# Attention heads laid as 64 partitions by 7 rows, on four 64x64 tiles of TensorE

## The chip, the cores and the metric

One core of one Trainium2 chip. The metric is the device time of one execution in microseconds (us), as the median of several; smaller is better. All runs told of here can be compared with one another. Each is set against runs of the kernel before in the same rounds.

## The reference

A cosine-similarity attention over 8 batches, 12 heads, 448 positions and 64 dimensions, followed by a two-layer perceptron with GELU over 3584 rows:

```python
q_n = q / (norm(q) + 1e-6);  k_n = k / (norm(k) + 1e-6)        # over the 64 dimensions
scores = q_n @ k_n.T / tau                                     # 448 x 448 per head
attn = exp(scores - max) / (sum + 1e-9)
x = (attn @ v), heads side by side: 3584 rows x 768
out = gelu(x @ w_in) @ w_out                                   # 768 -> 2048 -> 768
```

## The kernel before

Every batch has two stages. In the **attention stage** the heads go in pairs, each head's 448 positions as 112 partitions by 4 rows. GpSimd squares q and k and multiplies them by reciprocal norms, DMA transposes the result (TensorE does so in batch 0), TensorE makes scores, ScalarE exponentials, TensorE row sums and values, VectorE the division. Between groups of scores TensorE works off pieces of the second layer of earlier batches, the filler. The **first-layer stage** multiplies by `w_in`, and ScalarE makes the GELU. The parts that matter here:

```python
def scores(g, c0, n=2):                       # two heads = two row tiles of 64, keys in chunks of 112
    for c in range(c0, c0 + n):
        for h in range(2):
            nc.tensor.matmul(st[:CS, h, :S], lhsT=qkT[rows(h), 1, c, :], rhs=qkT[rows(h), 0, :, :], ...)
        nc.scalar.activation(pt, st[:CS, :, :S], AF.Exp, scale=inv_tau)

def columns(g, n, ...):                       # n=0: row sums; n=1, 2: odd and even halves of v
    ...                                       # four column tiles of 32: (head pair j, head h)
    nc.tensor.matmul(bank_t[g, n][r:r + 32, :S], lhsT=w, rhs=pt_t[g + j, c][:, h, :], tile_position=(0, r))

def reciprocals(g):
    nc.vector.transpose(tr, sums)             # 32x32 blocks
    nc.vector.reciprocal(rc, tr[:, :, 0])
    nc.vector.transpose(rs, rc.to_broadcast(...))

def normalise(g):
    for n in (2, 1):                          # the bank borrowed from the filler is freed first
        nc.vector.tensor_tensor(x_t[b][:, p + n - 1, :], bank_t.pop((g, n))[:, :S], rs, ALU.mult)

# attention stage, cut: filler of 96 or 128 matmuls in pieces, 16 to a bank, two banks by turns
plan = {96: ((18, 8), (8, 8), (0, 10), (8, 8), (0, 10), (8, 10)), 128: ...}
...
if i in (2, 4): both(g - 2, ...)              # sums, reciprocals, values, normalise
upto(reduce, ...)                             # next batch's squares: behind the normalising
```

## Time and profile before

| | before |
|---|---|
| median | 438.94 us (438.43 to 439.7) |
| TensorE busy | 428.9 us, 98% of the span |
| ScalarE, GpSimd, VectorE busy | 264.4, 204.3, 164.6 us |
| first layer of batch 0 starts at | 38.9 us |
| from one first layer to the next | 48.8 us (odd batches), 53.6 to 54.1 (even) |

TensorE's busy share is the first thing to read, and then whether it waits: in the waits of the kernel before (total us, times, longest), its longest wait after 60 us is 0.2 us:

```profile
PE hp L433 <- DVE x L246: 0.2, 1, 0.2
```

The chain of work is therefore a price list of TensorE's pieces. Those lines are in the prediction.

### The profile page before, as it was taken

The page shows a single profiled execution, that of the slowest core. Times are in us where ns is not written, and L with a number is a line of the kernel's source. Part 1 is how long each engine was busy: PE and PEld are TensorE (multiplying, and loading weights), DVE is VectorE, ACT ScalarE, POOL GpSimd, SP SyncE. Part 2 cuts the span into 40 slices and gives each one's busy share as a digit, 9 for nine tenths or more (in the row PEclk, how much of TensorE's full clock was granted, in tenths as well). Part 3 has the DMA queues.
Part 4 walks back from the last instruction along what each step waited for, and adds up shares of the span by engine and source line. Part 5 has one row for each costly group of instructions (what it writes and reads, how often), then busy time and mean ns, then how long its engine had stood idle before and what let it go on. Part 6 is the DMA issues. An engine that isn't in the chain of part 4 may idle for free.

```text
span 438.5 us, 7921 instructions
## 1 busy us (share of the span) xinstructions
PE 428.9 (98%) x3291; PEld 216.1 (49%) x3291; DVE 164.6 (38%) x266; ACT 264.4 (60%) x380; POOL 204.3 (47%) x185
## 2 busy tenths in 40 slices
PE   8899999999999999999999999999999999999996
PEld 4344544445444554455544545445444554445563
DVE  5667313642255305542154501753055421341021
ACT  4696587646766467754767359655766457773300
POOL 3989934491834609291571906655190732300000
PEclk9699999999999999999999999999999999999999
DMA  8999999945683907756195743858077600711022
GB/s 204 250 247 206 196 137 208 264 100 147 99 168 86 212 23 115 170 106 162 24 158 139 154 113 48 173 125 207 1 130 152 134 2 1 132 43 31 1 72 72
DMA packets 83635, 54.97 MB, mean 125 GB/s; under 512 B 41872, under 2 KB 78608, under 8 KB 83600
## 3 DMA queue, kind: packets, MB, share of 16 engines
q1 hardware_dynamic: 66416, 42.35, 43.0%
q0 software_dynamic: 16784, 11.80, 18.5%
q8 instruction: 25, 0.41, 0.4%
q10 hardware_dynamic: 400, 0.33, 0.2%
q14 instruction: 10, 0.08, 0.1%
HBM read 45.61 MB, written 11.01 MB: 129 GB/s over the span
## 4 chain that ended last, share of the span: by engine, by line
PE 93%; DVE 2%; ACT 2%; POOL 1%; DMA 1%; issue 0%; DVEq 0%; POOLq 0%
PE op L268 35%; PE hp L433 33%; PE st L206 12%; PE o L228 8%; PE sm L228 4%; ACT pt L209 1%; POOL qkb L176 1%; DMA qk<-in_q_dram 1%; PE spin L323 1%; PE tp L192 1%; DVE x L246 0%; DVE nq L147 0%; DVE nq L149 0%; ACT lq L155 0%; POOL v L120 0%
## 5 line engine op out<-in xcount | busy, mean ns | idle before, releaser
L209 ACT ACTIVATE pt<-st 112x896 bf16<-112x896 f32 x192 | 165.2, 913 | 49.6 <-PE st L206 49.2
L268 PE MATMUL op<-wo,g 128*128 128x384 bf16 x896 | 158.0, 327 | 0.0
L433 PE MATMUL hp<-x,wi 128*128 128x448 bf16 x768 | 147.0, 353 | 0.2 <-DVE x L246 0.2
L455 ACT ACTIVATE g<-hp 128x448 bf16<-128x448 f32 x128 | 67.0, 545 | 89.9 <-PE hp L433 89.5
L268 PEld LDWEIGHTS <-g 128*128 128x128 bf16 x896 | 81.8, 98 | 70.1 <-issue 21.0
L433 PEld LDWEIGHTS <-wi 128*128 128x128 bf16 x768 | 74.3, 98 | 72.3 <-issue 3.6
L176 POOL TENSOR_TENSOR qkb<-qk,rn 112x512 bf16<-112x512 f32 x95 | 97.8, 1055 | 11.3 <-DVE rn L167 11.0
L137 POOL TENSOR_TENSOR sq<-qk 112x1024 f32<-112x1024 f32 x44 | 82.3, 1888 | 5.8 <-DMA qk<-in_k_dram 5.7
L165 POOL TENSOR_SCALAR se<-sr 112x48 f32<-112x48 f32 x14 | 4.6, 326 | 150.0 <-ACT sr L164 150.0
L149 DVE TENSOR_REDUCE nq<-sq 112x16 f32<-112x1024 f32 x47 | 56.9, 1213 | 37.3 <-POOL sq L137 37.3
L206 PE MATMUL st<-qkT 64*112 64x448 bf16 x384 | 60.9, 380 | 1.9 <-ACT pt L209 1.7
L279 DVE COPY ot<-op 128x384 f32<-128x384 f32 x55 | 29.8, 542 | 79.3 <-PE op L268 79.3
L167 DVE RECIPROCAL rn<-se 112x48 f32<-112x48 f32 (+1 forms) x20 | 7.8, 392 | 99.7 <-POOL se L165 99.4
L228 PE MATMUL o<-pt,v 112*32 112x448 bf16 x768 | 41.4, 353 | 0.2 <-DVE x L246 0.2
L206 PEld LDWEIGHTS <-qkT 64*112 64x112 bf16 x384 | 21.7, 126 | 38.4 <-issue 34.9
L246 DVE TENSOR_TENSOR x<-o,rs 128x448 bf16<-128x448 f32 x48 | 27.7, 619 | 4.3 <-PE o L228 2.0
L235 DVE STREAM_TRANSPOSE tr<-sm 128x448 f32<-128x448 f32 x24 | 15.5, 647 | 35.5 <-PE sm L228 35.5
L228 PEld LDWEIGHTS <-v 112*32 112x32 bf16 x768 | 20.3, 97 | 16.0 <-issue 1.1
L228 PE MATMUL sm<-pt,ones 112*32 112x448 bf16 x384 | 23.1, 355 | 0.0
L239 DVE STREAM_TRANSPOSE rs<-rc 128x448 f32<-128x448 f32 x24 | 15.5, 645 | 0.8
L323 PE MATMUL spin<-blank,ident 112*112 112x448 bf16 x43 | 14.1, 483 | 1.5 <-POOL ident masks.py:199 1.3
L120 POOL DMA_DIRECT2D v<-in_v_dram x17 | 14.0, 822 | 0.0
(37 smaller groups left out, 80.6 us busy)
## 6 DMA issues: line engine op xcount, KB each, us to landing
qk<-in_q_dram SPq DMA_DIRECT2D x48, 224.0 KB, 5.9
qk<-in_k_dram SPq DMA_DIRECT2D x47, 224.0 KB, 6.1
v<-in_v_dram POOLq DMA_DIRECT2D x15, 336.0 KB, 6.9
wi<-in_moe_w_in_dram POOLq DMA_DIRECT2D x4, 768.0 KB, 9.6
wo<-in_moe_w_out_dram POOLq DMA_DIRECT2D x4, 768.0 KB, 16.9
out_dram<-ot SPq DMA_DIRECT2D x7, 336.0 KB, 3.6
out_dram<-ot SPq DMA_DIRECT2D x8, 288.0 KB, 2.6
out_dram<-ot SPq DMA_DIRECT2D x8, 240.0 KB, 2.7
```

The source lines that it names most:

```text
L137: nc.gpsimd.tensor_tensor(sq, t, t, ALU.mult)
L149: nc.vector.tensor_reduce(nq, sq, mybir.AxisListType.X, ALU.add)
L176: eng.tensor_tensor(qkb[:, i].rearrange("p c h d -> p h c d"), t[:, i], rn[:, i].to_broadcast([CS, 2, NC, D]), ALU.mult)
L206: nc.tensor.matmul(st[:CS, h, :S], lhsT=qkT[rows, 1, c, :], rhs=qkT[rows, 0, :, :], start=True, stop=True)
L209: nc.scalar.activation(pt, st[:CS, :, :S], AF.Exp, scale=inv_tau)
L228: nc.tensor.matmul(bank_t[g, n][r:r + 32, :S], lhsT=w, rhs=pt_t[g + j, c][:, h, :], start=(c == 0), stop=(c == NC - 1), tile_position=(0, r))
L246: nc.vector.tensor_tensor(x_t[b][:, p + n - 1, :], bank_t.pop((g, n))[:, :S], rs, ALU.mult)
L268: nc.tensor.matmul(ps[:, :NH], lhsT=g_t[sb][:, kf, t * 128:(t + 1) * 128], rhs=wo[:, kf, ni * NH:(ni + 1) * NH], start=(kf == 0), stop=(kf ...
L279: nc.vector.tensor_copy(ot[:, lo:hi], ps[:, :NH])
L323: nc.tensor.matmul(ps[:CS, :S], lhsT=ident, rhs=blank, start=True, stop=True)
L433: nc.tensor.matmul(hps[m], lhsT=wi[:, kd, m * 128:(m + 1) * 128], rhs=x_t[b][:, kd, :], start=(kd == order[0]), stop=(kd == order[-1]))
L455: nc.scalar.activation(g_t[sb][:, m, hf * S:(hf + 1) * S], hps.pop(m), AF.Gelu)
```

## The change

Its intent: a head's positions become 64 partitions by 7 rows, so that two heads fill 128 partitions. Four heads (a quad) then fill the array as four 64x64 tiles, both in the scores and in the values, with all 128 lanes of ScalarE and no partition idle. A sum of a head lands in two 32-partition quadrants, one for even and one for odd key chunks, so VectorE must add the halves of neighbouring quadrants. The core of it, cut:

```diff
-    CS = S // 4                                   # 112 partitions x 4 rows, pairs of heads
+    C = S // D                                    # 64 partitions x 7 rows, quads of heads
 def scores(...):
+        for n, (s, c) in enumerate(banks):
+            for h in range(2):
+                nc.tensor.matmul(st[cols, n, :S], lhsT=qkT[rows, 1, c, cols], rhs=qkT[rows, 0, :, cols],
+                                 start=True, stop=True, tile_position=(64 * s, 64 * h))
+    def sums(g, chunks=range(C)):                 # ones: columns 0-15 for rows 0-63, 16-31 for rows 64-127
+                r = 32 * (2 * s + c % 2)
+                nc.tensor.matmul(bank_t[g, "sm"][r:r + 32, :S], lhsT=ones, rhs=pt_t[g, s, c], ...)
+    def values(g, chunks=range(C), aside=0):
+                    nc.tensor.matmul(bank_t[g, h][cols, :S], lhsT=v_t[g][rows, s, c, :],
+                                     rhs=pt_t[g, s, c][rows], tile_position=(64 * h, 64 * s), ...)
 def reciprocals(g):
     transpose -> tr
+        for j in range(4):
+            nc.vector.tensor_copy(sw[32 * j:32 * (j + 1)], sums2[32 * (j ^ 1):32 * ((j ^ 1) + 1)])
+        nc.vector.tensor_tensor(su, sums2, sw, ALU.add)
+        nc.vector.reciprocal(rc, su)
+        for h in range(2): transpose rc[:, h] -> rs       # two instead of one
 def normalise(g):
-        for n in (2, 1):
+        for h in range(2):                        # the filler's bank is freed last
 attention stage:
+        plan = {96: (0, 18, 8, 8, 8, 0, 8, 8, 0, 8, 8, 22), 128: (0, 22, 12, 12, 12, 0, 12, 12, 0, 12, 12, 22)}
+            if i in (5, 8): both(...)
+            group(b, i)
+            if i in (4, 9): upto(reduce, ...)     # at 4: ahead of the first sums
```

(Cut: loads, stores and `w_in` in the new order, quad-sized squares and scaling, and the schedule of batch 0.)

## The prediction

> **What bounds the kernel now.** I read the page's busy table first, then the chain of work that ended last, in order of time, then the timelines of single engines around one attention batch. The page:
>
> ```profile
> PE 428.9 (98%) x3291; PEld 216.1 (49%) x3291; DVE 164.6 (38%) x266; ACT 264.4 (60%) x380; POOL 204.3 (47%) x185
> ...
> PE 93%; DVE 2%; ACT 2%; POOL 1%; DMA 1%; issue 0%; DVEq 0%; POOLq 0%
> ```
>
> TensorE is the bound: busy 98% of the span and 93% of the chain. Only the first batch, up to 38.97 us, has other links in the chain. So a change pays by taking matmul time out, and costs by making TensorE wait. The chain inside one later batch (number 3 of 0 to 7) gives the prices:
>
> ```profile
> 160.06 0.52 PE st L206 x4
> 160.57 3.03 PE op L268 x18
> 163.61 0.52 PE st L206 x4
> 164.12 1.41 PE op L268 x8
> ...
> 170.24 0.87 PE sm L228 x16
> 171.10 1.51 PE o L228 x32
> 172.62 0.52 PE st L206 x4
> 173.13 1.73 PE op L268 x10
> ```
>
> The 32 value matmuls take 1.51 us: four column tiles at once make 8 rounds of 0.189 us, a 448-column matmul's time. The 16 row sums take 0.87, 4 rounds (0.76) and 0.11. A score group of 4 (two row tiles, 2 rounds, 0.38) takes 0.52, so 0.14 over; 8 output-projection matmuls (`op`) take 1.41, 1.30 and 0.11. Every change of tile shape thus costs 0.11 to 0.14 us. The `op` matmuls of the previous batches are the filler between score groups, and they accumulate 16 to a bank, in two banks by turns.
>
> VectorE and GpSimd are not the bound, but two of their chains run close behind TensorE. VectorE after the first row sums of batch 3:
>
> ```profile
> 171.16 0.65 DVE L235 STREAM_TRANSPOSE tr<-sm 128x448 f32<-128x448 f32 x1 [3.19 <-PE sm L228]
> 171.84 0.24 DVE L237 RECIPROCAL rc<-tr 128x14 f32<-128x14 f32 x1
> 172.12 0.65 DVE L239 STREAM_TRANSPOSE rs<-rc 128x448 f32<-128x448 f32 x1
> 172.87 1.16 DVE L246 TENSOR_TENSOR x<-o,rs 128x448 bf16<-128x448 f32 x2
> 173.94 1.21 DVE L149 TENSOR_REDUCE nq<-sq 112x16 f32<-112x1024 f32 x1
> ```
>
> The sums start at 170.16 in TensorE's timeline, so `tr` starts 1.00 us later and both normalising multiplies are over 3.87 us after the start. The first multiply frees the bank that the next filler chunk needs; the reduction of the next batch's squares is issued only after them. And GpSimd in the same stretch:
>
> ```profile
> 165.21 2.04 POOL L176 TENSOR_TENSOR qkb<-qk,rn 112x512 bf16<-112x512 f32 x2 [0.57 <-DVE rn L167]
> 167.20 0.83 POOL L120 DMA_DIRECT2D v<-in_v_dram  x1
> 168.04 2.05 POOL L176 TENSOR_TENSOR qkb<-qk,rn 112x512 bf16<-112x512 f32 x2
> 170.05 1.89 POOL L137 TENSOR_TENSOR sq<-qk 112x1024 f32<-112x1024 f32 x1
> ```
>
> Its scaling starts 5.15 us after the attention batch (160.06), released by the reciprocal norms; 512 elements take 1.0 us start to start and 1024 squares 1.85.
>
> **What the Trainium skill says.** "TensorEngine Tiling (Array Packing)", Key Properties: changing the tiling mode drains the engine. The trace agrees: 0.11 to 0.14 us at each change. "TensorE: Matmul & The Clock Gate", Part 3: row and column tiles compose and run at once. The trace shows either kind alone at full overlap (rows in the scores, columns in the values), not both together. The same page, Part 1: an idle time over a free-running window of about 3.4 us can halve the clock. The trace's granted clock did fall, to 0.70 between 15 and 25 us, after the sparse first scores. "VectorE: DVE Perf Modes", Two Vector instructions with no wait between them: an instruction whose input or output starts in another 32-partition quadrant than the last one's is held until earlier ones finish. The kernel before has no such copies, so it cannot show this; the change adds four in a row.
>
> **The change, part by part.**
>
> TensorE. Two heads by four 112-key chunks become four heads by seven 64-key chunks. Per batch, scores go from 24 rounds to 21 and values from 24 to 21, if four 64x64 tiles run at once. Score groups: before 12 of 0.52 = 6.24 us; after ten of 0.52 and one of one round, 0.33, = 5.53: −0.71. One filler piece fewer: −0.11. Sums: 14 matmuls on four column tiles still need 4 rounds: 0. Values: 7 rounds are 1.32, plus a new shape change after the sums (0.11) and some exposed weight loading (0.03, estimated): 1.46 against 1.51, −0.05, three times. Together about −1.0 us per batch, −7 us for batches 1 to 7.
>
> ScalarE: 168 exponentials of 128x896 for 192 of 112x896 at 913 ns, −22 us of busy time. It is hidden behind TensorE in batches 1 to 7 but counts in batch 0: three fewer at 0.82 us back to back is −2.4. Against it, GpSimd now works on whole quads there (scaling 896 elements: 1.75 us by 512 -> 1.0; squares of 1792: 3.25), and the second quad's scaling ends later. I take batch 0 as −1 ± 2.
>
> VectorE after the sums. The first transpose stays (0.65 + 0.03). New: four copies of 28 elements across quadrants, one addition, a reciprocal of 28 instead of 14, a second transpose. The trace has a reduction from 32 to 16 elements at 179 ns and a 16-element reciprocal at 253 ns; I estimate 0.22 start to start for each held copy and for the addition, and 0.36 for the reciprocal (253 ns for 16 and 452 ns for 48 give 6.2 ns per element). Then 0.60 and 0.72 for two transposes and 1.16 for two multiplies. From the sums' start: 1.00 + 0.68 + 0.88 + 0.22 + 0.36 + 0.60 + 0.72 + 1.16 = 5.62 us, against 3.87.
>
> **Where that meets TensorE.** Values of the second head in each pair go to the idle filler bank, which is the one the next chunk of `op` needs, and it is now freed by the last multiply, not the first. In odd batches the filler has used 18+8+8+8 = 42 matmuls when the first sums come and 58 at the second: each time 6 are left to a multiple of 16. In even batches it is 22+36 = 58 (6 left) and 82 (14 left). From the sums' start TensorE needs 0.87 + 1.46 + 0.52 and 6 x 0.163 = 0.98, so at 3.83 us it wants the bank, which comes at 5.67 with the semaphore. **A wait of 1.84 us**, twice in odd batches and once in even ones (with 14 left TensorE wants it after 5.7 us or later). The kernel before escaped it: its first multiply ended at 3.3 against about 3.9.
>
> Worse, the reduction of the next batch's first squares now stands ahead of the first `tr` in VectorE's order. On batch 3's clock: scaling 165.1 to 168.6 (2 x 1.75), squares to 171.9, reduction (1792 elements, 2.02 us by 1213 ns for 1024) to 174.0. `tr` wanted to start at 171.1, so it is 2.9 us late and **the first wait of an odd batch is 4.8 us**. In an even batch the longer filler starts the sums about 2.3 us later (16 more matmuls by 0.163, less 0.3 for the groups' waits), `tr` is some 0.6 late, and the wait is 2.4. At the batch's end, 16 first-layer matmuls (3.03 us) stand between values and the last operands: 0.87 + 1.46 + 0.11 + 3.03 = 5.47 against 5.67, perhaps 0.1 to 0.2 lost.
>
> Sum: four odd batches x (4.8 + 1.84 + 0.15) = 27.2; three even x (2.4 + 0.15) = 7.7. Minus 7, minus 1: +27. 438.9 + 27 = **466 us**. A wait of 4.8 us may also halve the clock for some microseconds, four times; I put that into the range, not into the number.
>
> **Rivals.** (1) The matmul saving alone decides: about 431 us, −1.9%, if VectorE's chain kept ahead. For it: TensorE's 93% of the chain. Against it: 3.83 against 5.67 us, a margin that no plausible copy cost closes; copies at half the price still leave 1.4. (2) Only the bank waits occur, without the late reduction, because squares finish earlier than I think: 11 x 1.84 + 1 − 8 gives about 453. Against it: GpSimd's start is set by the roots, whose place in the order does not change. (3) Four tiles do not overlap fully, since two column tiles with different moving data share 64 rows: rounds up to doubled would add 42 x 0.19 = 8 us per batch, so 500 or more. Against it: four column tiles with four moving operands already overlap. I give it 5%.
>
> **Range and chances.** 466 with 8 in 10 between 448 and 480: the low end is rival 2 with cheaper copies, the high end colder clocks and dearer copies. Faster by over 2% needs both waits absent and a good batch 0: 0.06. Within 2%: 0.10. Slower: 0.84.
>
> **What will show it.** Right: `op` waiting for `x` about eleven times, four of them near 5 us; `tr` released by the reduction rather than the sums in odd batches; VectorE 5 us from `tr` to the last multiply's end where nothing is in the way; seven score rounds of 0.19 per quad; ScalarE near 242 us. Wrong: `op` never waiting for `x`, squares done before the first sums, or a score group over 0.6 us, which would mean tiles one after another.

## The result

The outputs are correct. **The changed kernel takes 536.02 us (median of 4, 534.5 to 537.71) against 439.27 us for the kernel before in the same rounds: ratio 1.220, 95% interval 1.217 to 1.223.** A ratio here is the mean time of one kernel's runs over that of the other's in the same rounds, so it is not quite the ratio of the medians. The direction was forecast, the size was not: 536 lies far outside 448 to 480.

The changed kernel's page (busy time, granted clock in 40 slices, then groups with busy us, mean ns and the idle time ahead of them):

```profile
PE 439.4 (82%) x3428; PEld 211.9 (40%) x3428; DVE 243.7 (46%) x387; ACT 242.9 (46%) x351; POOL 171.5 (32%) x113
PEclk9568999888999899797999989979799998999999
L451 PE MATMUL hp<-x,wi 128*128 128x448 bf16 x768 | 161.6, 373 | 34.1 <-DVE x L266 34.1
L287 PE MATMUL op<-wo,g 128*128 128x384 bf16 x896 | 162.8, 333 | 31.1 <-DVE x L266 31.1
L253 DVE COPY sw<-tr 32x28 f32<-32x28 f32 x96 | 72.3, 753 | 1.8
```

TensorE has fallen from 98% to 82%, and two groups of matmuls now wait 34 and 31 us for the normalised values `x`. VectorE has 79 us more work, and 72 of them are the four small copies: 753 ns for 28 elements. The clock granted to TensorE (`PEclk`, in tenths of full speed), full in the kernel before from the third slice on, dips all along. The waits (total us, times, longest):

```profile
PE hp L451 <- DVE x L266: 34.1, 6, 5.7
PE op L287 <- DVE x L266: 31.1, 11, 5.1
```

Eleven filler waits were forecast, the longest of about 5 us. The six of 5.7 us before the first layer were not. One of them, first in TensorE's timeline (start, length, times, idle time ahead), then in VectorE's, then in GpSimd's:

```profile
171.65 0.93 PE L230 MATMUL sm<-pt,ones 128*32 128x448 bf16 x14
172.52 1.52 PE L241 MATMUL o<-pt,v 64*64 64x448 bf16 x28
173.97 3.20 PE L451 MATMUL hp<-x,wi 128*128 128x448 bf16 x16
182.86 3.68 PE L451 MATMUL hp<-x,wi 128*128 128x448 bf16 x9 [5.69 <-DVE x L266]
```

```profile
172.63 0.65 DVE L249 STREAM_TRANSPOSE tr<-sm 128x448 f32<-128x448 f32 x1 [0.31 <-PE sm L230]
173.31 7.18 DVE L253 COPY sw<-tr 32x28 f32<-32x28 f32 x4
180.53 0.20 DVE L255 TENSOR_TENSOR su<-tr,sw 128x28 f32<-128x28 f32 x1
```

```profile
170.69 6.63 POOL L187 TENSOR_TENSOR qkb<-qk,rn 128x896 bf16<-128x896 f32 x4 [0.62 <-DVE rn L176]
177.28 3.17 POOL L147 TENSOR_TENSOR sq<-qk 128x1792 f32<-128x1792 f32 x1
```

Four copies of 28 elements take 7.18 us while GpSimd works through its scalings and a set of squares. The single copies take 0.75, 1.63, 1.64 and 3.11 us: each but the first is about one GpSimd instruction long, and each ends 0.03 to 0.05 us after a GpSimd instruction does. In the last batch GpSimd has nothing to do, and the same four take:

```profile
476.09 0.65 DVE L249 STREAM_TRANSPOSE tr<-sm 128x448 f32<-128x448 f32 x1 [3.50 <-PE sm L230]
476.78 0.75 DVE L253 COPY sw<-tr 32x28 f32<-32x28 f32 x4
```

The account of the profiled runs, 532.7 against 438.5 us: batch 0 takes 16.8 us more (its first layer starts at 55.7), the filler waits are 31.1, the first-layer waits 34.1, and 90 first-layer and filler matmuls after 35 us started at about half the usual rate, 15.2 us in all. Seven batches of saved matmuls are −7 (the forecast; run 9 below bears it out). That makes 90 of 94.

### The profile page after: what moved, and what is told of

It reads as the page before. It is cut to its first block, busy times and chain, and to the rows that moved or that the text cites. A ratio compares the mean times of both kernels' runs of the same rounds, so it can differ in the third digit from the quotient of the medians.

```text
span 532.7 us, 8122 instructions
## 1 busy us (share of the span) xinstructions
PE 439.4 (82%) x3428; PEld 211.9 (40%) x3428; DVE 243.7 (46%) x387; ACT 242.9 (46%) x351; POOL 171.5 (32%) x113
## 4 chain that ended last, share of the span: by engine, by line
issue 44%; PE 23%; POOL 21%; DVE 8%; DMA 2%; ACT 1%; SPq 0%; POOLq 0%; DVEq 0%
PE hp L451 10%; POOL sq L147 10%; POOL qkb L187 9%; PE op L287 8%; DVE sw L253 4%; PE st L216 2%; PE o L241 1%; PE sm L230 1%; DMA qk<-in_k_dram 1%; ACT pt L220 1%; DVE rs L260 1%; POOL v L127 1%; DVE nq L157 1%; DVE x L266 1%; DVE tr L249 1%
## 5 line engine op out<-in xcount | busy, mean ns | idle before, releaser
L220 ACT ACTIVATE pt<-st 128x896 bf16<-128x896 f32 x168 | 145.2, 914 | 102.8 <-PE st L216 102.3
L451 PE MATMUL hp<-x,wi 128*128 128x448 bf16 x768 | 161.6, 373 | 34.1 <-DVE x L266 34.1
L287 PE MATMUL op<-wo,g 128*128 128x384 bf16 x896 | 162.8, 333 | 31.1 <-DVE x L266 31.1
L187 POOL TENSOR_TENSOR qkb<-qk,rn 128x896 bf16<-128x896 f32 (+1 forms) x48 | 79.1, 1674 | 13.8 <-DVE rn L176 13.8
L253 DVE COPY sw<-tr 32x28 f32<-32x28 f32 x96 | 72.3, 753 | 1.8
L147 POOL TENSOR_TENSOR sq<-qk 128x1792 f32<-128x1792 f32 x22 | 69.9, 3178 | 0.2
L216 PE MATMUL st<-qkT 64*64 64x448 bf16 x672 | 56.8, 386 | 3.2 <-ACT pt L220 2.8
L157 DVE TENSOR_REDUCE nq<-sq 128x28 f32<-128x1792 f32 (+2 forms) x26 | 48.3, 1861 | 23.6 <-POOL sq L147 23.5
L241 PE MATMUL o<-pt,v 64*64 64x448 bf16 x672 | 38.4, 361 | 12.7 <-DVE qkT L206 12.1
L216 PEld LDWEIGHTS <-qkT 64*64 64x64 bf16 x672 | 17.5, 109 | 35.9 <-issue 30.5
L241 PEld LDWEIGHTS <-v 64*64 64x64 bf16 x672 | 18.8, 109 | 30.2 <-issue 21.4
L230 PE MATMUL sm<-pt,ones 128*32 128x448 bf16 x336 | 23.9, 371 | 0.4 <-ACT pt L220 0.4
```

What stands on the lines that cost most here:

```text
L147: nc.gpsimd.tensor_tensor(sq, t, t, ALU.mult)
L157: nc.vector.tensor_reduce(nq[:, part], sq[:, part], mybir.AxisListType.X, ALU.add)
L187: eng.tensor_tensor(qkb[:, i, :, s0:s1].rearrange("p c s d -> p s c d"), t[:, i, s0:s1], rn[:, i].to_broadcast([128, s1 - s0, C, D]), ALU. ...
L216: nc.tensor.matmul(st[cols, n, :S], lhsT=qkT[rows, 1, c, cols], rhs=qkT[rows, 0, :, cols], start=True, stop=True, tile_position=(64 * s, 6 ...
L220: nc.scalar.activation(pt[:, :m], st[:, :m, :S], AF.Exp, scale=inv_tau)
L230: nc.tensor.matmul(bank_t[g, "sm"][r:r + 32, :S], lhsT=ones, rhs=pt_t[g, s, c], start=(c < 2), stop=(c >= C - 2), tile_position=(0, r))
```

## The experiments

**The theories.** *A*: a VectorE copy within SBUF needs a port that GpSimd uses too, and waits for the GpSimd instruction in hand. This is what the Trainium skill's "SBUF — State Buffer", Who interferes with whom, states: a copy may enter a 2-port mode and then the later of it and GpSimd is fully blocked; an operation with two SBUF inputs contends with a GpSimd instruction that reads SBUF; a `tensor_reduce` never contends. I had not drawn on that page in the prediction. The runs can show who waits for whom and for how long; that a port is the reason is the page's word, and no run here shows the mode in which a copy ran. *B*: moving data across quadrants is slow by itself. *C*: the order (the reduction ahead of the first transpose, the filler's bank freed last) costs most of it.

**1. The copies written as reductions.** The same moves, same quadrants, same order, but as a sum over an axis of one element:

```diff
-            nc.vector.tensor_copy(sw[32 * j:...], sums2[32 * (j ^ 1):...])
+            nc.vector.tensor_reduce(sw[32 * j:...], sums4[32 * (j ^ 1):...], X, ALU.add)   # sums4: [.., 1]
```

> The changed kernel with its four quadrant copies in VectorE written as reductions over an axis of one element: same data, same quadrants, same order. Theory A (a VectorE copy within SBUF waits for the GpSimd instruction in hand, since it wants a port that the two engines share): the four take 0.18 to 0.2 us each everywhere, the first layer no longer waits 5 to 6 us for x, batch 0 gets back some 9 us, and the time falls from 536 to about 465 (455 to 480), near the blind prediction. Rival B (any instruction that crosses quadrants is slow or held here): the four stay as long, 530 to 540 us. Rival C (the late reduction and the order in which banks are freed cause most of the loss): falls by under 10 us.

Measured: 485.77 us, ratio to before 1.104 (1.101 to 1.108). The 96 moves fall from 72.3 to 18.4 us, 192 ns each, with GpSimd busy or not, and TensorE's first-layer waits fall from 34.1 to 5.1 us. B is refuted, and A holds in what it says of waits: **50 of the 97 us hung on the copies' waits for GpSimd**, with the waits and slow matmuls that followed from them.

```profile
PE hp L453 <- DVE x L268: 5.1, 12, 0.7
```

It did not reach the expected 465, nor the range of 455 to 480. A part of that, 6 us by run 2, is that the addition, with two SBUF inputs, is caught in the copies' place; another is batch 0, whose first layer still starts at 53.2 us. VectorE's timeline of the same place in this run:

```profile
163.60 0.81 DVE L254 TENSOR_REDUCE sw<-tr 32x28 f32<-32x28 f32 x4
164.44 1.56 DVE L257 TENSOR_TENSOR su<-tr,sw 128x28 f32<-128x28 f32 x1
```

It takes 0.20 us where GpSimd is idle, 1.56 here, 4.90 once in batch 0.

**2. The addition with one input too.** A short reduction puts the own half beside the partner's, another adds the pair:

```diff
-        nc.vector.tensor_tensor(su, sums2, sw, ALU.add)
+        nc.vector.tensor_reduce(sw[:, :, :, 1], sums4, X, ALU.add)
+        nc.vector.tensor_reduce(su, sw, X, ALU.add)                      # sw: [128, 2, 14, 2]
```

> As the run before, and the addition of two SBUF operands is a reduction over a pair as well, with one more short reduction to bring the own half beside the partner's. Theory A with the addition also caught by the port: the addition of the run before is sometimes over 1 us, and this run is 5 to 15 us faster than it. Theory A with the addition free: it is 0.2 us in both, and this run is within 3 us of the one before, rather slower by the extra instruction. Rival B: 530 to 540 us.

Measured: 479.51 us, 1.090 (1.087 to 1.094), 6.3 less than the run before, in spite of one instruction more. All five moves and the sum stay at 0.2 us. TensorE no longer waits before the first layer; the filler still waits 11 times:

```profile
PE op L290 <- DVE x L269: 26.6, 11, 4.1
```

In odd batches the next batch's reduction still stands ahead of the first transpose. VectorE in batch 3, whose last sum matmul starts at 190.46:

```profile
191.28 2.02 DVE L157 TENSOR_REDUCE nq<-sq 128x28 f32<-128x1792 f32 x1 [3.59 <-POOL sq L147]
193.22 0.64 DVE L249 STREAM_TRANSPOSE tr<-sm 128x448 f32<-128x448 f32 x1
```

First layer of batch 0: 50.0 us.

**3. The kernel before with the four copies.** They are put behind its first transpose; nothing reads their result.

```diff
 def reciprocals(g):                               # kernel before
     nc.vector.transpose(tr, sums)
+    for j in range(4):
+        nc.vector.tensor_copy(sw[32 * j:32 * (j + 1)], sums2[32 * (j ^ 1):32 * ((j ^ 1) + 1)])
```

> The kernel before, with the same four quadrant copies put behind the first transpose and their result not used. Theory A: GpSimd is busy there in most batches, so copies wait for its 1.0 and 1.9 us instructions one after the other, 3 to 6 us per set where GpSimd is busy, and the time rises from 439 to 470 to 510 us with TensorE waiting for x. Rival B as slow crossing as such: a similar rise but the copies are equally long where GpSimd is idle (last batch). Neither: 4 x 0.19 us, within the slack of the kernel before, 439 to 442 us.

Measured: 507.0 us, 1.153 (1.150 to 1.156). Not one matmul is different, and 67 us are lost. One set, in VectorE's timeline and then GpSimd's:

```profile
196.76 6.72 DVE L239 COPY sw<-tr 32x28 f32<-32x28 f32 x4
```

```profile
196.82 2.03 POOL L176 TENSOR_TENSOR qkb<-qk,rn 112x512 bf16<-112x512 f32 x2
198.82 3.73 POOL L137 TENSOR_TENSOR sq<-qk 112x1024 f32<-112x1024 f32 x2
```

Here the first copy alone took 5.82 us: GpSimd, whose instructions followed each other without a gap, went through all of them before it got in. In the last two sets, with GpSimd done, a copy takes 0.18 us.

**4. Its control: the kernel before with the moves as reductions.**

```diff
-        nc.vector.tensor_copy(sw[32 * j:...], ...)
+        nc.vector.tensor_reduce(sw[32 * j:...], ..., X, ALU.add)
```

> The control of the kernel before with copies: the same four quadrant moves, unused, written as one-element reductions. Theory A (the shared port): 0.18 to 0.2 us each whatever GpSimd does, 0.8 us a set, inside the slack of about half a microsecond to one and a half at the filler bank and the first layer, so 439 to 443 us against 507 with copies. Rival B (moves across quadrants): about 500 us again.

Measured: 444.19 us, 1.010 (1.008 to 1.012), 1 us above what was expected.

```profile
173.71 0.82 DVE L239 TENSOR_REDUCE sw<-tr 32x28 f32<-32x28 f32 x4
```

Runs 3 and 4 are the case in small: the same moves cost 4 us in one instruction and 67 in another. The lengthening of VectorE's chain by 0.8 us is nearly, not quite, hidden.

**5. The order alone, copies as they are.** The first multiply frees the filler's bank, the first layer takes its last two operands in that order, the reduction goes behind the normalising:

```diff
-        for h in range(2):                        # second transposes, and multiplies
+        for h in (1, 0):
-            if i in (4, 9): upto(reduce, ...)
+            if i in (5, 9): upto(reduce, ...)
```

> The changed kernel with its copies as they are, but the filler bank freed by the first multiply, the first layer taking its last two operands in that order, and the next batch's reduction issued after the normalising. Rival C (order is the cause): falls to 445 to 470 us. Theory A: the copies still wait for GpSimd, the waits before the first layer stay near 5 us, and the time falls by 5 to 25 us only, to 510 to 530.

Measured: 529.24 us, 1.203 (1.199 to 1.206): 7 us less than the changed kernel. C is not the main cause. While the copies wait for GpSimd, an earlier start of the chain buys little: their own time rises, from 72.3 to 79.6 us.

**6. One-input instructions and the order together** (the edits of 2 and 5).

> The run with one-input instructions only, plus the order: bank freed by the first multiply, reduction after the normalising. Theory: the first sums of odd batches no longer lose 2.4 us behind the reduction, each of 11 filler waits is 4.48 - 3.10 = 1.4 us, together 15 us instead of 26.6, and fewer cold clocks: 479.5 falls to 460 (455 to 467). Rival (the order matters little because the waits are set by the number of VectorE instructions alone): 472 to 478.

Measured: 456.79 us, 1.039 (1.037 to 1.042). The same edit that brought 7 us over the changed kernel brings 23 here. The filler waits are 11 of at most 1.2 us, 13.4 in all, and no matmul after 35 us is slow any more; in run 2, with waits up to 4.1 us, 41 were, 5.9 us in all. In the changed kernel the slow matmuls come behind the nine waits of 5.1 us and more, 6 to 15 behind each, and behind none of those of 2.9 and 1.5 us. In run 2 they also come behind two of its waits of 1.7 to 1.9 us. So the slow clock follows long waits, but these runs give no length from which it does.

**7. Batch 0 in another order.** Two reductions of batch 1 move behind the normalising of batch 0, so that they no longer stand ahead of transpose copies:

```diff
-            if c == 3: upto(reduce, 5)            # and likewise reduce 6, from c == 3 to c == 4
+            if c == 5: upto(reduce, 5)
```

> As e6_both, and in batch 0 the two early reductions of batch 1 stand after the normalising instead of ahead of transpose copies that TensorE waits for. Theory: TensorE's wait of 5 us in the values of the first quad goes, the first layer starts 5 to 8 us sooner than at 50 us, total 5 to 8 us less than e6_both. Rival (batch 0 is bound by GpSimd's scaling of whole quads): less than 2 us.

Measured: 456.45 us, 1.037 (1.033 to 1.041): nothing gained, where 5 to 8 us were expected. Batch 0's first layer starts at 43.7 instead of 49.6 us, as the theory has it, but batch 1 takes 57.3 instead of 50.0: its first scores now wait 3.6 us for a DMA transpose, and slow matmuls follow. The gain was given back.

**8. The filler split otherwise**, so that at each set of sums 15 matmuls are left to fill the open bank, instead of 6 (14 at the second set of an even batch):

```diff
-        plan = {96: (0, 18, 8, 8, 8, 0, 8, 8, 0, 8, 8, 22), 128: (0, 22, 12, 12, 12, 0, 12, 12, 0, 12, 12, 22)}
+        plan = {96: (0, 22, 9, 9, 9, 0, 8, 8, 0, 8, 8, 15), 128: (0, 26, 13, 13, 13, 0, 8, 8, 0, 12, 12, 23)}
```

> As e7_batch0_order, with the filler split so that 15 matmuls instead of 6 are left in the open bank at each set of sums. Theory: TensorE wants the bank 9 x 0.163 = 1.5 us later, the 1.4 us waits all go, 15 to 20 us less than e7_batch0_order, about 437 (430 to 443), which would leave the 7 us of saved matmul time to be seen in batches 1 to 7 (48.0 and 52.8 us for 48.8 and 53.8). Rival (something else bounds the batches): stays above 448.

Measured: 443.51 us, 1.009 (1.007 to 1.011), 13 less than the run before (15 to 20 were expected); the filler waits are gone from the list. Batches 2 to 7 take 52.7 (even) and 47.6 us (odd; 47.1 the last). The range was missed by half a microsecond at the top, because batch 1 still takes 55.0: TensorE waits 4.6 us for the transpose, issued at 51 and landed at 67 us.

**9. The second half of `w_out` loaded behind that transpose.**

```diff
-        upto(load_wo, 4)                          # first-layer stage, ahead of ...
         for n in (nu + 1, nu + 2): upto(scale, n); upto(transposes, n)
+        upto(load_wo, 4)
```

> As e8_filler_plan, and the second half of the second layer's weights is loaded after the first transposes of batch 1 are on their way. Theory: in e8 the first scores of batch 1 wait 4.6 us for a DMA transpose that is issued at 51 us and lands at 67, next to weight loads that land at 61 and 67; with those loads behind it the transpose lands before the first layer of batch 0 ends (62 us), the period of batch 1 falls from 55.0 to about 48 to 50 us and the total to 436 to 439. Rival (the transpose is slow for another reason, such as the loads of the next heads or its own size): unchanged, 442 to 445.

Measured: 437.96 us against 439.11 for the kernel before, **0.9974 (0.9961 to 0.9988): faster than both kernels**, by a quarter of a per cent. Batch 1 takes 48.7 us, and no wait for a transpose is left. There are no slow matmuls after 35 us. Pieces of batch 4 in its chain of work:

```profile
210.86 0.50 PE st L216 x8
...
218.42 0.50 PE st L216 x8
...
224.36 0.88 PE sm L230 x14
...
242.93 0.86 PE sm L230 x14
243.80 1.45 PE o L241 x28
```

Eight score matmuls are two rounds of four tiles in 0.50 us; the values' 28 are seven rounds in 1.45, shape change included. The tiles do run four at once.

**10. Squares of the second quad's keys on ScalarE in batch 0** (on top of 9).

```diff
-            nc.gpsimd.tensor_tensor(sq[:, 1], t[:, 1], t[:, 1], ALU.mult)
+            nc.scalar.activation(sq[:, 1], t[:, 1], AF.Square)
```

> As e9_later_weights, and the second quad's key squares in batch 0, 896 elements, move from GpSimd, where they stand 3.1 us ahead of the second scaling, to ScalarE. Theory: the second scaling starts about 1 us sooner and the first layer starts at 41.5 to 42.5 us instead of 42.8: 0.5 to 1.5 us less than e9. Rival (GpSimd's later whole-quad scaling bounds batch 0): no change within 0.4 us.

Measured: 438.13 us, 0.9977 (0.9964 to 0.9989), first layer at 43.4 us as in run 9: no difference. This part of GpSimd's work was not what batch 0 waited for; what is, in the 4.5 us that it still takes more than before, was not settled.

## Why the prediction was right or wrong

- **The step that failed is a term of the sum: "I estimate 0.22 start to start for each held copy and for the addition".** It was sized from a short reduction and a short reciprocal, which no run here shows lengthened beside GpSimd (the reciprocal takes 0.33 us in all 24 places of run 2). The four copies take 0.75 us a set where GpSimd is idle (0.19 each, so 0.22 was fair), but 2.0 us in the first set of batches 1 to 6 and 7.1 to 7.2 us in the third: 0.75 us a copy on average. The addition took its 0.20 in the changed kernel, because the copies had waited already. Experiments 1 and 2 put it at 50 + 6 of the 70 us missing. Written without the port, the kernel takes 479.5.
- From it followed the second failure: "perhaps 0.1 to 0.2 lost" before the first layer. That is where GpSimd scales the next batch, so the wait was 5.7 us there; in run 2 it is gone, as the arithmetic without the port would have it.
- **Batch 0, "−1 ± 2", was wrong too**: +16.8 as changed, still +11 in run 2, so 5.7 of it went with the held copies. The sum counted ScalarE's exponentials and GpSimd's scaling, and not that reductions of batch 1 stand ahead of transpose copies in VectorE's order, which cost another 5.9 us (run 7). The rest was not taken apart; run 9 still has 4.5.
- The low weight of a colder clock was a choice that failed: it was left out of the number, and cost 15 us, 5.9 in run 2. Runs 6 and 9, with no wait over about 1.2 us in batches 2 to 7, have no slow matmul there.
- **Right: the matmul saving.** −1.0 us a batch was forecast; batches of run 9 take 47.6 and 52.7 us against 48.8 and 53.6. That rests on the pieces: values 1.45 in the last set (forecast 1.46; 1.49 is the mean of three), sums 0.86 to 0.88, a score group 0.50 (0.52). The odd batches save a little more than forecast because "12 of 0.52" was a misreading: their score groups before sum to 6.77 us and not 6.24, since four of the twelve take 0.62 or 0.76. Rival 3, tiles in turn, is refuted. ScalarE's 242.9 us were forecast as 242.
- **Right: that the bank waits come, and their number, eleven. Their sizes agree partly by luck.** In the changed kernel the longest is 5.1 us, but its first set of copies was held for 1.3 us; in run 2 the longest is 4.1 (4.8 forecast). Three are of that size and not four: the sum counted batch 7, which has no next batch whose reduction could delay it. The reduction did delay the first transpose of odd batches: it starts 2.76 us after the last sum matmul starts instead of 0.40, so 2.4 us late (2.9 forecast); moving it is part of run 6's 23 us (the lines stand at run 2). In run 2 the filler waits sum to 26.6 us, where the forecast's terms sum to 34 (4 x 6.64 + 3 x 2.4).
- Right by luck: run 2's batches 1 to 7 take 27.9 us more than before, as the forecast's sum for them (+28). The waits were smaller than forecast, and the slow matmuls (5.9 us) filled most of the place.
- Slips without weight: the chain of the kernel before leaves TensorE not only in the first batch, but also from 85.4 to 91.4 us, at the end of batch 1; and the terms of rival 2 add up to 452, not 453.

## What to carry to other kernels

Before a small VectorE instruction goes onto a path that TensorE waits for, ask what GpSimd is doing at that moment: a copy within SBUF, or an operation with two SBUF inputs, can last as long as GpSimd's instructions, while a reduction over one element does the same move unhindered. When a change lengthens a side chain, compare the moment when the bank is freed with the moment when TensorE asks for it, and move that moment (order, filler plan) with the change. A layout that saves 1 us a batch can be right and still lose 97 us by what it puts on the engines beside it.

## What the Trainium skill lacked or had wrong

- "SBUF — State Buffer", Who interferes with whom, agrees with the runs: copies 0.17 to 0.18 us alone and up to 5.8 us beside GpSimd; one-element reductions 0.19 us in both cases; the addition of two SBUF inputs 0.20 and 1.56 us. It lacks which engine is next when GpSimd's instructions follow each other without a gap. In some sets a copy gets in after each of them (0.75, 1.63, 1.64, 3.11 us), in others it waits through several (5.82 us in run 3, through four more than the one in hand). What decides between the two, no run here shows.
- "VectorE: DVE Perf Modes", Two Vector instructions with no wait between them: the kernel before could not show held copies; the changed one has them at 0.19 us start to start where GpSimd is idle, each starting after the last one's end. That agrees, and the page gives no duration for it.
- "TensorEngine Tiling (Array Packing)", Key Properties, gives no price for a change of mode. In the chains of the kernel before and of run 9 it is 0.10 to 0.14 us in most places, among four shapes; one to four score groups of a batch take 0.1 to 0.24 us more, and why was not looked into.
